# Output stores of a residual-quantizer codec kernel moved from GpSimd's queue to SyncE's, with retuned instruction order

## The chip, the cores and the metric

The kernel runs on one core of a Trainium2 chip. The metric is the device time of one execution in microseconds, from the first instruction to the last, of which the median over several executions is taken. One further execution was recorded by the hardware profiler, and all readings of engines, waits and transfers come from it.

## The reference

Two sequences of 16,000 frames with 512 channels pass through a three-tap depthwise filter and a SiLU. Then each frame is quantized in four rounds: find the nearest of eight codebook vectors, add it to the sum, subtract it from the residual. The sum passes through a second three-tap depthwise filter. All tensors are bf16.

```python
B, T, D, K = 2, 16000, 512, 3      # x: [B, T, D]; dw_enc, dw_dec: [K, D]
Nq, C = 4, 8                       # codebooks: [Nq, C, D]

xp = jnp.pad(x, ((0,0),(1,1),(0,0)))
z = sum(xp[:, i:i+T, :] * dw_enc[i] for i in range(K))      # (written as a loop)
z = jax.nn.silu(z)
res, q = z, 0
for s in range(Nq):
    cb = codebooks[s]
    d2 = |res|^2 - 2 res.cb + |cb|^2                        # [B, T, C]
    sel = cb[d2.argmin(-1)]
    q = q + sel
    res = res - sel
qp = jnp.pad(q, ((0,0),(1,1),(0,0)))
y = sum(qp[:, i:i+T, :] * dw_dec[i] for i in range(K))
```

## The kernel before

Each sequence is cut into tiles of up to 16 groups of 128 frames, 18 tiles in all. In a tile, partition p holds G neighbouring frames, so that a shift by one frame is a shift by one group slot. The channels have to lie on the partitions for the first filter; therefore x is loaded by transposing transfers, one for each group, and one more for each of the two halo slots at the ends (the frame before and the frame after). Two XT buffers take turns, so the load of tile n can begin when the taps of tile n - 2 have read their slots.

```python
SIZES = ([6, 8] + [16] * 7, [16] * 7 + [8, 6])
...
NX, NE, NZ, NOH, NY = 2, 3, 4, 4, 4          # buffers of XT, EX, Z, OHW, YB
...
def load(st):
    ...
    def one(g):
        nc.sync.dma_start_transpose(out=X[:, :, g + 1, :], in_=src[g])
    for g in range(G):
        add("SP", 1.56 if n < 2 else 1.36, ("load", n, 0.01 * g), lambda g=g: one(g), [], [("X", n % NX, g + 1)], tail=1.5)
    ...
    if t0 and n:       # halo in front: one more transposing transfer; else a memset and a copy on GpSimd
        ...
        add("SP", ..., lambda: nc.sync.dma_start_transpose(out=X[:, :, 0, :], in_=before), [], xe, tail=1.5)
    ...
```

In `front` the three taps are multiplied on VectorE (some on ScalarE) and added into Z; ScalarE makes the exponential, VectorE or ScalarE adds 1, ScalarE takes the reciprocal and VectorE multiplies it in (the SiLU). `select` computes the first three choices from scores (PE, VectorE), `resid` subtracts the three chosen vectors from Z in PSUM with one or two matmuls per block, after which either ScalarE copies the sum back (the matmul with the identity has added Z) or VectorE adds it to Z; then comes the fourth choice.

```python
def evac(zg=zg, box=box):
    v = ps(box)[:, 0:GH * P].rearrange("p (k c) -> p k c", c=P)
    if box["dest"] == "ACT":
        nc.scalar.copy(zg, v)
    else:
        nc.vector.tensor_tensor(out=zg, in0=zg, in1=v, op=ALU.add)
```

`windows` lays the one-hot choices of neighbouring frames beneath each other (OHW), and `back` makes the output from them by matmul with codebook times filter. ScalarE copies two groups at a time from PSUM into one of four YB buffers, and after two such copies the buffer is stored. The frames that two tiles share belong to one of them only; a store is therefore cut into pieces (112 partitions, 15 partitions, one partition and the like).

```python
def back(st):
    ...
    for k0 in range(0, GH, 2):
        ks = range(k0, min(k0 + 2, GH))
        y = ycount[0] % NY
        ycount[0] += 1
        Y = YB[y]
        for k in ks:
            ...
            add("ACT", act_psum(1024), key, lambda ...: nc.scalar.copy(Y[...], ps(box)), [], [("Y", y)], free=box, after=[j])
        add("POOL", 1.0, ("back", n, ks[-1] / GH), lambda Y=Y, g0=2 * k0, g1=2 * (ks[-1] + 1): store(st, Y, g0, g1), [("Y", y)], [],
            tail=5.0)

def store(st, Y, g0, g1):
    ...
    for p0, p1, lo, hi in split:
        nc.gpsimd.dma_start(out=view[p0:p1, lo:hi, :], in_=Y[p0:p1, lo - g0:hi - g0, :])
```

None of these calls issues at once. `add` notes a step with its engine, an assumed cost, its reads and writes and a rank; `Plan.order` then plays the steps through in a list scheduler with assumed costs and fixes the order in which every engine gets its instructions, and which engine takes the either-or steps. The weights `WHEN` set the rank of each kind of step in the first, the middle and the last tiles, `SHARE` and `SLACK` tilt the either-or choices, and `QUOTA` bounds how many PSUM blocks may wait for ScalarE or VectorE at a time. Where the scheduler sees PE idle it puts in filler matmuls (`fill`).

```python
rank = self.when[kind][part][0] + tile + self.when[kind][part][1] * place_in_tile      # shortened

def fill(j, k):
    for _ in range(k):
        nc.tensor.matmul(PS[j // 2][...], lhsT=IDENT, rhs=MSK.rearrange("p u w -> p (u w)"), start=True, stop=True)
```

Of the kernel before, what the change touches and what calls it, by code (L numbers as in the profile page):

```python
# [12 lines left out]
ACT = mybir.ActivationFunctionType  # L13
# [3 lines left out]
class Plan:  # L17
# [16 lines left out]
    def add(self, engine, cost, key, fn, reads=(), writes=(), take=None, free=None, hold=None, tail=0.0, after=(), dest=None, box=None, mm=0):  # L34
        n = len(self.steps)
        deps = set(after)
        for t in reads:
            if t in self.writer:
                deps.add(self.writer[t])
            self.readers.setdefault(t, []).append(n)  # L40
        for t in writes:
            if t in self.writer:
                deps.add(self.writer[t])
            deps.update(self.readers.get(t, ()))
            self.writer[t] = n
            self.readers[t] = []
        deps.discard(n)
        self.steps.append({"n": n, "e": engine, "c": cost, "k": key, "fn": fn, "deps": sorted(deps), "take": take, "free": free,
                           "hold": hold, "tail": tail, "dest": dest, "box": box, "mm": mm})
        return n  # L50
# [163 lines left out]
def kernel(  # L214
# [8 lines left out]
    nc = tc.nc  # L223
# [18 lines left out]
    PAIR = 1  # L242
    NX, NE, NZ, NOH, NY = 2, 3, 4, 4, 4
    NA = 4
    SHARE = (14.72, 0.75, -2.14)
    SLACK = (-0.24, -0.33, 0.67)
    QUOTA = {"ACT": 3, "DVE": 3}
    WHEN = {"setup": ((-0.151, 1.058), (0.208, 0.715), (-0.18, 0.669)), "load": ((-2.06, 0.878), (-1.99, 0.738), (-2.049, 0.878)),
            "pad": ((-1.379, 0.11), (-1.748, 0.188), (-2.303, 0.134)), "taps": ((0.021, 0.468), (-0.351, 0.479), (0.529, 1.222)),
            "exp": ((0.71, 0.323), (0.67, 0.275), (1.338, 0.094)), "plus1": ((1.243, 0.705), (0.347, 0.188), (-0.701, 0.508)),  # L250
            "recip": ((0.436, 0.72), (0.457, 0.028), (1.338, 0.536)), "gate": ((-0.006, 0.57), (0.836, 0.447), (1.306, 0.596)),
            "score0": ((-0.317, 0.008), (1.329, 0.132), (-0.226, 0.443)),
            "decide": ((1.768, 0.496), (0.086, 0.144), (0.22, 0.967)), "win0": ((2.207, 0.092), (2.21, 0.191), (2.978, 0.013)),
            "resid": ((1.259, 0.51), (1.669, 0.629), (1.801, 0.77)), "score3": ((2.134, 0.811), (2.579, 0.199), (3.141, 1.501)),
            "decide3": ((1.343, 0.361), (2.686, 0.74), (3.558, 0.652)), "win3": ((3.257, 0), (3.131, 1.109), (4.061, 0.121)),
            "back": ((2.863, 0.379), (3.366, 1.486), (4.147, 0.457))}
    assert B == len(SIZES) and T >= GM * P and GM <= 16

    xf = x.flatten_outer_dims()
# [65 lines left out]

    plan = Plan(NA, (3, len(tiles) - 3), SHARE, SLACK, QUOTA, WHEN)
    add = plan.add

    def ps(box):
        j = box["banks"][0]  # L330
        return PS[j // 2][:, 512 * (j % 2):512 * (j % 2 + len(box["banks"]))]
# [7 lines left out]
    def act_psum(n):  # L339
        return 0.055 + n / 1200  # L340

    def mm(n):
        return max(0.06, 0.004 + n / 2380)
# [398 lines left out]
    def back(st):  # L742
        n, GH = st["n"], st["GH"]
        W = OHW[n % NOH]
# [6 lines that stand above are left out]
                box = {}  # L751
                key = ("back", n, k / GH)

                def mms(k=k, box=box):
                    py = ps(box)
                    for u in range(2):
                        o = py[:, 512 * u:512 * u + 512]
                        wrap = (k == 0 and u == 0) or (k == GH - 1 and u == 1)
                        nc.tensor.matmul(o, lhsT=W[:, k, PADC:PADC + P], rhs=WDEC[u], start=True, stop=not wrap)  # L759
                        if wrap and u == 0:  # L760
                            nc.tensor.matmul(o, lhsT=W[:, GH - 1, PADC - 1:PADC - 1 + P], rhs=WDEC[2], start=False, stop=True)
                        elif wrap:
                            nc.tensor.matmul(o, lhsT=W[:, 0, PADC + 1:PADC + 1 + P], rhs=WDEC[3], start=False, stop=True)
                wraps = (k == 0) + (k == GH - 1)
                j = add("PE", (2 + wraps) * mm(512), key, mms, [("OHW", n % NOH, 0), ("OHW", n % NOH, 1)] + [("WDEC", v) for v in range(4)], [],
                        take=("A", box), dest="ACT", mm=2 + wraps)
                add("ACT", act_psum(1024), key, lambda k=k, box=box, Y=Y, k0=k0: nc.scalar.copy(  # L767
                    Y[:, 2 * (k - k0):2 * (k - k0) + 2, :].rearrange("p g d -> p (g d)"), ps(box)), [], [("Y", y)], free=box, after=[j])
            add("POOL", 1.0, ("back", n, ks[-1] / GH), lambda Y=Y, g0=2 * k0, g1=2 * (ks[-1] + 1): store(st, Y, g0, g1), [("Y", y)], [],
                tail=5.0)  # L770

    def store(st, Y, g0, g1):
        r0, a, e, G = st["row0"], st["a"], st["e"], st["G"]
        view = outf[r0:r0 + G * P, :].rearrange("(p g) d -> p g d", g=G)
        runs = []
        for p in range(P):
            lo = max(a - G * p, g0)
            hi = min(e - G * p, g1)
            if lo >= hi:
                continue  # L780
            if runs and runs[-1][2:] == [lo, hi]:
                runs[-1][1] = p + 1
            else:
                runs.append([p, p + 1, lo, hi])
        split = []
        for p0, p1, lo, hi in runs:
            m = (p1 - p0) // 16 * 16
            split += [(p0, p0 + m, lo, hi)] * (m > 0) + [(p0 + m, p1, lo, hi)] * (p0 + m < p1)
        for p0, p1, lo, hi in split:
            nc.gpsimd.dma_start(out=view[p0:p1, lo:hi, :], in_=Y[p0:p1, lo - g0:hi - g0, :])  # L790

    load(tiles[0])
    setup()
    for group in GROUPS:
        halves = {}
        for st in group:
            if st["n"]:
                load(st)
            for h in range(2):
                halves[st["n"], h] = front(st, h)  # L800
        for st in group:
            for h in range(2):
                front2(st, h, *halves[st["n"], h])
        for st in group:
            select(st)
            resid(st)
            back(st)
# [40 lines left out]
```

## Time and profile before

| what | value |
|---|---|
| median of 3 executions | 739.47 us (739.02 to 741.46) |
| span of the profiled execution | 739.7 us |
| mean granted TensorE clock | 0.949 |
| store issues on GpSimd (L790) | 130, 78.0 us busy |
| transposing loads on SyncE | 283 |
| data in the stores' queue | 32.78 MB in 10,640 packets |
| data in the loads' queue | 37.13 MB in 153,952 packets |
| time from a store's issue to its landing | 1.6 / 3.9 / 9.0 us (min / median / max) |

The profile's page gives for each engine its busy time and its share of the span; for groups of equal instructions the line, the engine, output and input, the count, the busy time and the mean duration; and the chain of work that ended last, followed back from the last instruction. "issue" stands for time in which an engine waited for nothing that the profile shows. PE is TensorE's matmul part, DVE is VectorE, ACT is ScalarE, POOL is GpSimd and SP is SyncE; a q behind the name is the engine's sequencer, which issues transfers. Durations of neighbouring instructions overlap a little, so their sum is above the busy time. Times behind a start are microseconds from the beginning of the span.

### The profile page before, as it was taken

How to read it: one execution, taken by the hardware profiler on the slowest of the kernel's cores; microseconds unless marked ns; L12 is line 12 of the kernel's file. 1: busy time of each engine (PE TensorE's matmuls, PEld its weight loads, DVE VectorE, ACT ScalarE, POOL GpSimd, SP SyncE). 2: the span in 40 equal slices, each digit the busy share in tenths (PEclk: the TensorE clock that was granted, in tenths of full speed). 3: DMA queues.
4: the chain of work that ended last, by engine and by line, in shares of the span. 5: the costliest groups of instructions: out<-in, count | busy, mean ns of one | idle time of the engine just before them, and what ended most of it. 6: DMA issues, size and time to landing. Idle time of an engine off the chain costs nothing.

```text
span 739.7 us, 24411 instructions
## 1 busy us (share of the span) xinstructions
PE 599.6 (81%) x10732; PEld 293.0 (40%) x10732; DVE 673.9 (91%) x1257; ACT 656.1 (89%) x584; POOL 90.0 (12%) x165
## 2 busy tenths in 40 slices
PE   5987977798689777876689969896788888899984
PEld 2443433345244333433245434443234444444441
DVE  8879798899999989998999999998799999899991
ACT  5677869899999979999899999999599999999664
POOL 2000000100040221103200011102101010201223
PEclk9998999899899999999899998999799999999997
DMA  5445544835182790629553292619523140203325
GB/s 112 91 98 130 101 89 86 133 69 88 30 187 44 117 179 8 131 62 182 95 101 74 54 184 72 109 50 209 111 57 87 37 91 2 88 32 115 116 84 182
DMA packets 164914, 71.89 MB, mean 97 GB/s; under 512 B 156640, under 2 KB 156672, under 8 KB 164808
## 3 DMA queue, kind: packets, MB, share of 16 engines
q1 hardware_dynamic: 153952, 37.13, 31.1%
q0 software_dynamic: 10640, 32.78, 14.5%
q8 instruction: 84, 1.38, 0.8%
q10 hardware_dynamic: 216, 0.43, 0.2%
q14 instruction: 22, 0.18, 0.1%
HBM read 0.43 MB, written 32.77 MB: 45 GB/s over the span
## 4 chain that ended last, share of the span: by engine, by line
DVE 52%; PE 20%; ACT 13%; issue 10%; DMA 2%; SPq 2%; POOL 1%; DVEq 0%; POOLq 0%; ACTq 0%
DVE ZB L710 12%; DVE ZB L365 9%; DVE TB L533 7%; ACT ZB L708 5%; PE ps L702 5%; DVE TA L365 5%; DVE TA L533 4%; PE ps L701 4%; PE ps L568 3%; PE ps L810 3%; ACT EX L550 3%; ACT EX L538 2%; DVE EX L540 2%; DVE OHW L679 2%; PE ps L759 2%
## 5 line engine op out<-in xcount | busy, mean ns | idle before, releaser
L702 PE MATMUL ps<-OHW,CBN 128*128 128x512 bf16 (+1 forms) x768 | 267.7, 387 | 14.8 <-DVE ZB L710 4.6
L708 ACT CAST ZB<-ps 128x1024 bf16<-128x1024 f32 (+2 forms) x290 | 248.8, 958 | 32.7 <-PE ps L702 32.5
L701 PE MATMUL ps<-ZB,IDENT 128*128 128x512 bf16 (+1 forms) x524 | 204.5, 390 | 22.2 <-DVE ZB L710 11.6
L710 DVE TENSOR_TENSOR ZB<-ZB,ps 128x1024 bf16<-128x1024 bf16 (+2 forms) x142 | 145.6, 1045 | 6.8 <-PE ps L702 6.1
L790 POOL DMA_DIRECT2D out_dram<-YB x130 | 78.0, 605 | 601.5 <-ACT YB L767 536.6
L767 ACT CAST YB<-ps 128x1024 bf16<-128x1024 f32 x126 | 123.1, 1052 | 12.8 <-PE ps L759 12.1
L538 ACT ACTIVATE EX<-ZB 128x4096 bf16<-128x4096 bf16 (+2 forms) x36 | 115.8, 3219 | 13.6 <-DVE ZB L365 13.5
L702 PEld LDWEIGHTS <-CBN 128*128 128x128 bf16 x768 | 75.9, 99 | 129.1 <-issue 61.1
L550 ACT ACTIVATE EX<-EX 128x4096 bf16<-128x4096 bf16 (+2 forms) x36 | 114.7, 3193 | 1.3 <-DVE EX L540 1.1
L568 PE MATMUL ps<-ZB 128*32 128x64 bf16 x8064 | 90.3, 197 | 13.8 <-issue 6.6
L568 PEld LDWEIGHTS <-ZB 128*32 128x32 bf16 x8064 | 76.9, 95 | 55.5 <-issue 52.8
L810 PE MATMUL ps<-MSK,IDENT 128*128 128x512 bf16 x307 | 81.2, 418 | 19.5 <-DVE RC L618 5.6
L533 DVE TENSOR_SCALAR TB<-XT,WENC 128x2048 bf16<-128x2048 bf16 (+2 forms) x140 | 94.1, 684 | 0.1
L759 PE MATMUL ps<-WDEC,OHW 128*128 128x512 bf16 x252 | 76.6, 395 | 13.1 <-DVE ZB L710 6.3
L701 PEld LDWEIGHTS <-IDENT 128*128 128x128 bf16 x524 | 52.5, 100 | 65.4 <-issue 13.8
L365 DVE TENSOR_TENSOR ZB<-ZB,EX 128x4096 bf16<-128x4096 bf16 (+2 forms) x36 | 72.6, 2019 | 3.7 <-ACT EX L550 3.7
L365 DVE TENSOR_TENSOR TA<-TA,TB 128x4096 bf16<-128x4096 bf16 (+2 forms) x36 | 72.7, 2018 | 0.1
L365 DVE TENSOR_TENSOR ZB<-TA,TB 128x4096 bf16<-128x4096 bf16 (+2 forms) x36 | 72.6, 2018 | 0.1
L810 PEld LDWEIGHTS <-IDENT 128*128 128x128 bf16 x307 | 30.9, 104 | 57.8 <-issue 31.0
L533 DVE TENSOR_SCALAR TA<-XT,WENC 128x2048 bf16<-128x2048 bf16 (+2 forms) x71 | 47.2, 682 | 0.2
L759 PEld LDWEIGHTS <-OHW 128*128 128x128 bf16 x252 | 23.3, 100 | 43.9 <-issue 22.2
L540 DVE TENSOR_SCALAR EX<-EX 128x4096 bf16<-128x4096 bf16 (+2 forms) x36 | 39.1, 1087 | 1.7 <-ACT EX L538 1.7
(100 smaller groups left out, 426.8 us busy)
## 6 DMA issues: line engine op xcount, KB each, us to landing
out_dram<-YB POOLq DMA_DIRECT2D x33, 448.0 KB, 3.8
out_dram<-YB POOLq DMA_DIRECT2D x28, 512.0 KB, 4.2
XT<-in_x_dram SPq DMA_TRANSPOSE x283
out_dram<-YB POOLq DMA_DIRECT2D x30, 60.0 KB, 4.7
out_dram<-YB POOLq DMA_DIRECT2D x31, 2.0 KB, 2.5
out_dram<-YB POOLq DMA_DIRECT2D x2, 224.0 KB, 3.9
YB<-in_dw_dec_dram ACTq DMA_DIRECT2D x1, 384.0 KB
out_dram<-YB POOLq DMA_DIRECT2D x1, 384.0 KB
```

Source lines behind the costliest of these rows:

```text
L365: add("DVE", cost, key, lambda: nc.vector.tensor_tensor(out=out, in0=a, in1=b, op=op), reads, writes, **kw)
L533: lambda dst=dst, src=src, w=w: nc.vector.tensor_scalar(out=dst, in0=src, scalar1=w, scalar2=None, op0=ALU.mult),
L538: add("ACT", act(2 * R), ("exp", n, h), lambda: nc.scalar.activation(v(ex), Z, ACT.Exp, scale=-1.0), zt, [("EX", sl), "ACTTAB"], hold="E")
L550: nc.scalar.add_instruction(mybir.InstActivation(name=nc.get_next_instruction_name(), engine=mybir.EngineType.Activation, func=ACT.Reciprocal,
L568: nc.tensor.matmul(o[HB * q:HB * (q + 1), u * ZW:(u + 1) * ZW].rearrange("p (s c) -> p s c", s=2), lhsT=blk, rhs=both, start=False, stop=( ...
L701: nc.tensor.matmul(o, lhsT=IDENT, rhs=zg[:, k0:k0 + nk, :], start=True, stop=False)
L702: nc.tensor.matmul(o, lhsT=CBN[s, u][:, i * P:(i + 1) * P], rhs=W[:, k0:k0 + nk, PADC:PADC + P], start=not on_act, stop=True)
L708: nc.scalar.copy(zg, v)
L710: nc.vector.tensor_tensor(out=zg, in0=zg, in1=v, op=ALU.add)
L759: nc.tensor.matmul(o, lhsT=W[:, k, PADC:PADC + P], rhs=WDEC[u], start=True, stop=not wrap)
L767: add("ACT", act_psum(1024), key, lambda k=k, box=box, Y=Y, k0=k0: nc.scalar.copy(Y[:, 2 * (k - k0):2 * (k - k0) + 2, :].rearrange("p g d ...
L810: nc.tensor.matmul(PS[j // 2][:, 512 * (j % 2):512 * (j % 2) + NMK * ZW], lhsT=IDENT, rhs=MSK.rearrange("p u w -> p (u w)"), start=True, s ...
```

## The change

The output stores are issued by SyncE, in the same queue as the transposing loads; GpSimd has nothing left to do after the setup but the few halo memsets and copies at the ends of the sequences. The loads and their halo slots are as before. [...]The scheduler's weights were tuned anew for the new queue (with 0.5 in place of 1.0 for a store's issue and 4.0 in place of 5.0 for its landing), so the order of instructions on all engines differs from before.

```diff
-    SHARE = (14.72, 0.75, -2.14)
-    SLACK = (-0.24, -0.33, 0.67)
-    QUOTA = {"ACT": 3, "DVE": 3}
-    WHEN = {"setup": ((-0.151, 1.058), (0.208, 0.715), (-0.18, 0.669)), "load": ((-2.06, 0.878), (-1.99, 0.738), (-2.049, 0.878)),
-            ... (all other kinds of steps)
+    SHARE = (19.5, 1.71, -1.34)
+    SLACK = (0.8, -4.83, -5.72)
+    QUOTA = {"ACT": 4, "DVE": 4}
+    WHEN = {"setup": ((-0.05, 1.675), (0.613, 1.016), (0.464, 0.931)), "load": ((-2.074, 0.741), (-2.063, 0.601), (-2.58, 0.741)),
+            ... (all other kinds of steps)
@@ back
-            add("POOL", 1.0, ("back", n, ks[-1] / GH), lambda Y=Y, g0=2 * k0, g1=2 * (ks[-1] + 1): store(st, Y, g0, g1), [("Y", y)], [],
-                tail=5.0)
+            add("SP", 0.5, ("back", n, ks[-1] / GH), lambda Y=Y, g0=2 * k0, g1=2 * (ks[-1] + 1): store(st, Y, g0, g1), [("Y", y)], [],
+                tail=4.0)
@@ store
-            nc.gpsimd.dma_start(out=view[p0:p1, lo:hi, :], in_=Y[p0:p1, lo - g0:hi - g0, :])
+            nc.sync.dma_start(out=view[p0:p1, lo:hi, :], in_=Y[p0:p1, lo - g0:hi - g0, :])
```

## The prediction

> **What bounds the kernel now.** I read the busy shares first. In the page's first part each engine has its busy time, its share of the span and its number of instructions:
>
> ```profile
> PE 599.6 (81%) x10732; PEld 293.0 (40%) x10732; DVE 673.9 (91%) x1257; ACT 656.1 (89%) x584; POOL 90.0 (12%) x165
> ```
>
> VectorE is busy 91% and ScalarE 89%: two engines share the bound. GpSimd, which the change empties, has 12%. VectorE's whole idle time is 739.7 - 673.9 = 65.8 us, which caps what a change can win that leaves VectorE its work. Next, the table by stretches (start:end, length, then busy time and instruction count of each engine, granted clock, DMA share, GB/s) says where the 65.8 us lie:
>
> ```profile
> 460.00:500.00 40.00, 34.74 (x785) 17.65 (x784) 39.84 (x52) 39.94 (x32) 3.90 (x6) 1.00 0.43 80
> 500.00:540.00 40.00, 27.23 (x510) 13.15 (x509) 33.04 (x78) 32.06 (x23) 6.87 (x13) 0.87 0.79 148
> 700.00:720.00 20.00, 17.91 (x274) 8.20 (x273) 18.28 (x48) 12.96 (x17) 3.62 (x7) 1.00 0.23 81
> 720.00:740.00 20.00, 8.66 (x134) 3.84 (x132) 4.81 (x14) 10.07 (x11) 7.80 (x15) 0.80 0.56 185
> ```
>
> 460 to 500 is the good middle: VectorE and ScalarE full. 500 to 540 is the worst middle stretch (7 us of VectorE idle). The last 20 us hold 15.2 us of VectorE idle: there the kernel only drains. Summing the same table, the first 100 us hold about 15 us, the last 40 about 17, the rest about 33.
>
> The chain that ended last says the same, and says how small the part of the changed engine is:
>
> ```profile
> DVE 52%; PE 20%; ACT 13%; issue 10%; DMA 2%; SPq 2%; POOL 1%; DVEq 0%; POOLq 0%; ACTq 0%
> ```
>
> GpSimd has 1% of it, about 7 us, SyncE's queue and the transfers 2% each. So stores cost the end nearly nothing until the tail. Then I read the two queues that the change joins. Issue durations (min/median/max ns) of the transposing loads on SyncE, of the store issues on GpSimd, and of one plain transfer issued by ScalarE through the same kind of queue as SyncE's:
>
> ```profile
> L494 SPq DMA_TRANSPOSE XT<-in_x_dram x252: 1188/1265/3319, 0.7 to 594.9; - x126
> L790 POOL DMA_DIRECT2D out_dram<-YB x130: 484/536/2732, 69.0 to 735.9; - x130
> L350 ACTq DMA_DIRECT2D YB<-in_dw_dec_dram x1: 356/356/356, 4.2 to 4.2; - x1
> ```
>
> SyncE's timeline in the middle shows its rhythm (start, length, instructions merged):
>
> ```profile
> 412.10 29.09 SPq L494 DMA_TRANSPOSE XT<-in_x_dram  x16
> 441.24 1.26 SPq L502 DMA_TRANSPOSE XT<-in_x_dram  x1
> 442.55 1.26 SPq L508 DMA_TRANSPOSE XT<-in_x_dram  x1
> 450.77 28.20 SPq L494 DMA_TRANSPOSE XT<-in_x_dram  x16
> ```
>
> One tile of 16 groups takes 18 issues; seven tiles from 198.19 to 490.59 us give a period of 41.8 us. Part of the 29 us is waiting: the chain of waits of SyncE has about 180 us of waits on VectorE (taps that still read the XT buffer) over the run. Last the tail, GpSimd's timeline:
>
> ```profile
> 723.97 1.57 POOL L790 DMA_DIRECT2D out_dram<-YB  x3 [1.53 <-ACT YB L767]
> 728.79 4.05 POOL L790 DMA_DIRECT2D out_dram<-YB  x8 [3.25 <-ACT YB L767]
> 735.43 1.07 POOL L790 DMA_DIRECT2D out_dram<-YB  x2 [2.58 <-issue]
> ```
>
> ScalarE's last copy starts at 731.1 and ends near 732.2; the last two stores issue only at 735.43, after 2.58 us [...], and the span ends at 739.7. The tail behind the last compute is 7.5 us.
>
> [...]issues have median 536 and maximum 2732 ns, so a few are held up, but no VectorE operation is: the 2048-element taps have a median of 746 and the longest tap into TB took 758 ns, into TA 894. [...]queue shares now are 31.1% (loads) and 14.5% (stores), which the change puts into one queue. [...]No run here shows SyncE stores yet. [...]The 180 us of SyncE waits are the reason why that may hurt.
>
> **The change part by part.** *Issue work.* 130 store issues leave GpSimd (78.0 us busy) and join SyncE's 283 transposes. At 0.36 us (the ScalarE sample) to 0.60 us (its slowest, the 3 KB load) they are 47 to 78 us on SyncE beside 283 x 1.265 = 358 us: 405 to 436 us, 55 to 59% of the span. Per period: 18 x 1.28 + 8 x 0.5 = 27 us of 41.8. SyncE isn't a bound by volume.
>
> *Order.* SyncE takes its list in order, so a store waits behind loads and a load behind stores. I compared the new SyncE order with its gates: for every load the last tap of the tile two before (in VectorE's order), for every store its last YB copy (in ScalarE's). Positions are sums of the mean durations of the rows by shape up to that instruction, each engine scaled to end near 720 to 725 us; read in the same way, before's stores come out 5 to 20 us ahead of the trace, both engines alike, so I shift both by 15. Example: the load of tile 10 stands behind the third store of tile 4. Store ready at 286 + 15 = 301, tap gate of tile 8 at 288 + 15 = 303: the store costs it nothing. The load then takes about 22 us to 325; tile 10's first tap stands at 337 + 15 = 352. Margin 27 us. Going through all 18 loads in this way, margins are 2 to 5 us for tiles 2 to 4 (no store ahead of them), about 15 for tiles 5 and 6, and 24 to 41 for tiles 7 to 17. From tile 3 on, a store that stands behind a load lags about 18 to 25 us, mostly one per tile, on the fourth YB buffer; that buffer is next written about 20 us after such a store. So neither side should close on the path: 0 us.
>
> *VectorE and ScalarE.* The two orders hold the same work but for flips of the either-or operations: VectorE gets 6 more OHW copies of 0.4 to 0.7 us and 5 more small OT copies, and loses 6 residual adds (4 x 0.68, 2 x 0.55) and some taps: -1 us. ScalarE gets 6 short casts, three short taps and one "plus 1" of 2048, and loses 6 OHW copies, 5 OT copies and a long tap: +1 us. PE loses 13 filler matmuls and gains 6 identity matmuls. Nothing here moves the bound.
>
> *Tail.* Only here are stores on the path. In the new order the last stores are again the pieces of the last two tiles. The issue of the last piece [...](3.2 us past the last copy) should shrink to about 1.5 as each issue is shorter [...]. I put it at -2 us (-1 to -3).
>
> *Retuned ranks.* Planner weights, the PSUM quota (3 to 4) and the store's assumed tail differ, so nearly every instruction has another place. The 33 us of middle idle can go either way. 13 fewer fillers mean that the planner saw a little less PE idle; I take -3 us from it, with a spread of 10.
>
> Sum: 739.5 - 2 - 3 + 0 = 734.5 us.
>
> **The rivals.** First, head-of-line blocking: ScalarE runs late, a store holds SyncE, and the next load is late for its taps. For it speaks that a store is placed ahead of most loads; against it the margins of 24 us and more. If half the 14 full tiles lost 3 us: +21, 758 us. Second, the opposite: a store stuck behind an 18-transpose load keeps a YB buffer and stops ScalarE. The trace has no ScalarE wait on a store among its listed waits, and one 2.64 us piece in the chain at 483.49; with lags of 18 to 25 us against reuse in about 20 to 30, a few waits of 1 to 3 us are possible: +5, 742 us. Third, GpSimd's silence frees VectorE. Against: VectorE durations show no tail; at most 1 us. Fourth, the retuned order fills the dips like 500 to 540: if half of the 33 us go, 718 us; nothing in the profile says that it must.
>
> **Range and chances.** The mechanical part is small and one-sided (-1 to -3); the reshuffle has about +-10, blocking a thin tail upwards. 8 in 10: 720 to 750. 2% is 14.8 us: faster means below 724.7, slower above 754.3. I give 0.18, 0.70 and 0.12.
>
> **What would show it.** Right: SyncE's loads keep a 1.26 us median, store issues on it take 0.35 to 0.6 us, no wait of VectorE's taps on XT transfers in the middle of the run, no YB wait on ScalarE beyond a few us, VectorE and ScalarE busy within 3 us of now, a tail behind the last copy of 5 to 6 us. Wrong: SyncE waiting on ScalarE's YB copies while VectorE idles for XT; landing times above 6 us as stores share a queue with transposes; store issues above 1 us, which would put SyncE near 70%; or a middle idle far from 33 us, which would be the reshuffle and not the stores.

## The result, and the profile after

The change makes the kernel 1.1% faster: 731.31 us median (730.0 to 732.07, four executions) against 739.25 us (736.4 to 741.46, four executions) of the kernel before in the same comparison, a ratio of 0.9893 with the interval 0.9856 to 0.993. The predicted time was 734.5 us with the range 720 to 750. As the runs below show, the size came out nearly right while the division of the sum between queue and order was wrong.

The profiled execution of the kernel after has a span of 729.5 us at a clock of 0.961. Busy times by engine, and the chain that ended last, on its page (its lines are numbered one lower than before: the store is L789, the load L493, the copy into YB L766):

```profile
PE 593.4 (81%) x10725; PEld 289.3 (40%) x10725; DVE 675.0 (93%) x1258; ACT 658.3 (90%) x583; POOL 10.7 (1%) x35
```

```profile
DVE 50%; PE 28%; ACT 10%; issue 8%; DMA 3%; SPq 1%; ACTq 0%; DVEq 0%
```

The work of VectorE and ScalarE is as before (+1.1 and +2.2 us); GpSimd has fallen from 90.0 to 10.7 us. So the 10.2 us between the two spans are idle time of VectorE that has gone: 729.5 - 675.0 = 54.5 us in place of 65.8. The table by stretches of the kernel after, in the columns of the prediction's table:

```profile
460.00:500.00 40.00, 31.71 (x443) 14.78 (x443) 38.78 (x64) 37.33 (x27) 0.00 (x0) 0.91 0.35 81
500.00:540.00 40.00, 33.46 (x714) 17.05 (x714) 37.29 (x62) 36.21 (x31) 0.00 (x0) 0.91 0.50 111
700.00:720.00 20.00, 18.75 (x309) 9.05 (x307) 16.36 (x42) 14.45 (x21) 0.00 (x0) 1.00 0.29 101
720.00:740.00 20.00, 1.90 (x8) 0.70 (x8) 0.23 (x1) 4.57 (x5) 0.00 (x0) 0.82 0.30 93
```

The worst middle stretch, 500 to 540, lost 7 us of VectorE before and loses 2.7 now; the best one lost 0.2 and loses 1.2. Next, the issue durations on SyncE (min/median/max ns, first and last start):

```profile
L493 SPq DMA_TRANSPOSE XT<-in_x_dram x252: 1189/1265/2552, 0.7 to 603.1; - x126
L789 SPq DMA_DIRECT2D out_dram<-YB x130: 227/370/1666, 96.5 to 725.1; - x130
```

The load's issue is unchanged (median 1.265 us). A store's issue takes 0.37 us where GpSimd took 0.54. SyncE's timeline shows what one queue means here: its 413 issues start one after another, none before the one ahead of it has ended, and stores and loads alternate in blocks.

```profile
404.66 12.97 SPq L789 DMA_DIRECT2D out_dram<-YB  x8
417.72 28.68 SPq L493 DMA_TRANSPOSE XT<-in_x_dram  x16
449.13 15.79 SPq L789 DMA_DIRECT2D out_dram<-YB  x12
```

Eight store issues of 0.4 us fill 13 us here because they wait for ScalarE's copies (8.8 us in three waits, the longest 6.7, and no load starts meanwhile). Last the tail, ScalarE's and SyncE's timelines:

```profile
715.94 10.50 SPq L789 DMA_DIRECT2D out_dram<-YB  x14
718.06 6.51 ACT L766 CAST YB<-ps 128x1024 bf16<-128x1024 f32 x7 [0.32 <-ACT YB L766]
```

The last copy ends at 718.06 + 6.51 = 724.6 us and the span at 729.5: a tail of 4.9 us, where it was 7.5. Before, GpSimd paused 2.58 us ahead of its last two issues; the profile names nothing that it waited for ("issue"), and what it was stays open. Here no such gap stands: SyncE's last two issues start at 724.4 and 725.1 us.

### The profile page after: what moved, and what is told of

Same layout as the page of the kernel before. It is cut to its first block, busy times and chain, and to the rows that moved or that the text cites. A ratio compares the mean times of both kernels' runs of the same rounds, so it can differ in the third digit from the quotient of the medians.

```text
span 729.5 us, 24386 instructions
## 1 busy us (share of the span) xinstructions
PE 593.4 (81%) x10725; PEld 289.3 (40%) x10725; DVE 675.0 (93%) x1258; ACT 658.3 (90%) x583; POOL 10.7 (1%) x35
## 3 DMA queue, kind: packets, MB, share of 16 engines
q8 instruction: 84, 1.38, 0.8%
## 4 chain that ended last, share of the span: by engine, by line
DVE 50%; PE 28%; ACT 10%; issue 8%; DMA 3%; SPq 1%; ACTq 0%; DVEq 0%
DVE ZB L709 12%; PE ps L701 8%; DVE ZB L364 7%; PE ps L700 7%; DVE TA L364 6%; DVE TB L532 6%; PE ps L567 5%; ACT YB L766 3%; DVE TA L532 3%; PE ps L758 3%; ACT ZB L707 2%; DVE EX L539 2%; DVE OHW L678 2%; PE ps L809 2%; ACT EX L549 1%
## 5 line engine op out<-in xcount | busy, mean ns | idle before, releaser
L707 ACT CAST ZB<-ps 128x1024 bf16<-128x1024 f32 (+2 forms) x296 | 253.5, 933 | 33.1 <-PE ps L701 32.0
L709 DVE TENSOR_TENSOR ZB<-ZB,ps 128x1024 bf16<-128x1024 bf16 (+2 forms) x136 | 143.0, 1063 | 4.7 <-PE ps L701 4.2
L766 ACT CAST YB<-ps 128x1024 bf16<-128x1024 f32 x126 | 121.8, 1045 | 9.0 <-PE ps L762 4.1
L567 PEld LDWEIGHTS <-ZB 128*32 128x32 bf16 x8064 | 75.2, 95 | 55.9 <-issue 52.4
L567 PE MATMUL ps<-ZB 128*32 128x64 bf16 x8064 | 87.5, 197 | 7.0 <-issue 4.2
L532 DVE TENSOR_SCALAR TB<-XT,WENC 128x2048 bf16<-128x2048 bf16 (+2 forms) x139 | 92.6, 684 | 0.2
L758 PE MATMUL ps<-WDEC,OHW 128*128 128x512 bf16 x252 | 74.0, 387 | 13.5 <-DVE ZB L709 4.5
L809 PE MATMUL ps<-MSK,IDENT 128*128 128x512 bf16 x294 | 73.7, 402 | 13.5 <-DVE RC L617 2.4
L700 PEld LDWEIGHTS <-IDENT 128*128 128x128 bf16 x530 | 53.0, 100 | 67.6 <-issue 15.9
L809 PEld LDWEIGHTS <-IDENT 128*128 128x128 bf16 x294 | 28.9, 102 | 47.5 <-issue 19.9
L758 PEld LDWEIGHTS <-OHW 128*128 128x128 bf16 x252 | 22.8, 98 | 41.7 <-issue 18.4
L561 PE MATMUL ps<-MSK,IDENT 128*128 128x512 bf16 (+1 forms) x64 | 24.5, 383 | 8.5 <-ACT ZB L707 2.4
```

The lines of the kernel that those rows point to most:

```text
L532: lambda dst=dst, src=src, w=w: nc.vector.tensor_scalar(out=dst, in0=src, scalar1=w, scalar2=None, op0=ALU.mult),
L567: nc.tensor.matmul(o[HB * q:HB * (q + 1), u * ZW:(u + 1) * ZW].rearrange("p (s c) -> p s c", s=2), lhsT=blk, rhs=both, start=False, stop=( ...
L700: nc.tensor.matmul(o, lhsT=IDENT, rhs=zg[:, k0:k0 + nk, :], start=True, stop=False)
L809: nc.tensor.matmul(PS[j // 2][:, 512 * (j % 2):512 * (j % 2) + NMK * ZW], lhsT=IDENT, rhs=MSK.rearrange("p u w -> p (u w)"), start=True, s ...
```

## The experiments

The change has two parts, the queue of the stores and the order of instructions. The first question was which of the two brought the 8 to 10 us. The theory followed the prediction: the queue moves only the tail, the retuned order does the rest. The rival: the queue does more than the tail, in the middle. Each ratio is to the kernel before as it ran in the same comparison: 740.82 us for the first four runs, 740.26 for the four with thin stores, 739.57 for the last four. One profiled execution stands behind each reading of idle time.

**Each part alone.** The order of before with all stores on SyncE:

```diff
-            nc.gpsimd.dma_start(out=view[p0:p1, lo:hi, :], in_=Y[p0:p1, lo - g0:hi - g0, :])
+            nc.sync.dma_start(out=view[p0:p1, lo:hi, :], in_=Y[p0:p1, lo - g0:hi - g0, :])
```

> The kernel before with its own order of PE, VectorE and ScalarE to the last instruction; only the 130 stores are issued by SyncE, merged into its loads by planned time. Theory (the queue is worth only its tail, the rest of the 8 us is the retuned order): about 736.5 us, ratio 0.995 to 0.998, the stretch behind ScalarE's last copy 5 us in place of 7.5. Rival 1 (the queue gives it all): 731 to 732, ratio 0.989. Rival 2 (an order that was not planned for it blocks SyncE): above 739.5, with VectorE waiting for XT.

The order of after with all stores on GpSimd (the same edit the other way round, in the kernel after):

> The changed kernel with its order of PE, VectorE and ScalarE to the last instruction; only the stores go back to GpSimd. Theory: about 734 us, ratio 0.992 to 0.995, tail again 7 to 7.5 us, the last copy still ends near 725 to 727. Rival 1 (the queue gives it all): 739. Rival 3 (the new order needs the freed buffers of the new queue): above 736 with ScalarE waiting for YB.

And the kernel after once more, in the same comparison:

> The changed kernel unchanged, on the same chip as the two halves: 731 us, ratio 0.989. Theory: its gain is the sum of the gains of the two halves within 2 us; if stores and order need each other, it is more than the sum.

Measured, with 740.82 us for the kernel before: queue alone 730.79 us, ratio 0.9861 (0.9838 to 0.9884); order alone 733.24 us, 0.9886 (0.9856 to 0.9916); both 731.48 us, 0.9871 (0.9845 to 0.9897). Either part alone gives the whole gain. If the two were independent, both together would give 0.9861 x 0.9886 = 0.975; the measured interval ends far above that. The two parts therefore remove for the most part the same loss. And the queue alone brings 10 us, of which the tail (7.5 to 5.5 us in this run) is only 2.

The order's part has a second rival, TensorE's granted clock: on average 0.963 in the six executions of the order alone, against 0.955 in the 27 of the kernel before and 0.956 in the six of the queue alone. Among those 27 a clock higher by 0.01 went with 2.1 us less (interval 0.5 to 3.7), so up to 3 of the order's 8 us may come with the clock. The queue's 10 us don't. No run held the clock fixed.

**Tail and middle apart.** The order of before, with the stores of the last two tiles on SyncE, and then its complement, all stores but those:

```diff
-            nc.gpsimd.dma_start(out=view[p0:p1, lo:hi, :], in_=...)
+            (nc.sync if st["n"] >= len(tiles) - 2 else nc.gpsimd).dma_start(...)     # last two tiles
+            (nc.sync if st["n"] < len(tiles) - 2 else nc.gpsimd).dma_start(...)      # the complement
```

> The kernel before, in which only the stores of the last two tiles are issued by SyncE. Theory: the same gain as with all stores on SyncE, 736.5 to 737.5, ratio 0.995 to 0.998, since only the tail of the stores is on the path. Rival: under 1 us of gain, so that any gain of all stores on SyncE comes from the middle.

> The order of the kernel before, with every store but those of the last two tiles on SyncE: the complement of the run that moved only the last two tiles' stores. Theory (the middle and the tail are separate gains): the whole queue change brought about 10 us, its tail part about 2, so this run should lie 7 to 8 us below the kernel before, ratio 0.988 to 0.992, with a tail behind the last copy of about 7 us as before. Rival (the gain of the middle is drift of the runs, or hangs on the tail's queue): within 3 us of before, ratio above 0.996.

Measured: the last two tiles alone 738.9 us, ratio 0.9973 (0.995 to 0.9995), with a tail of 5.2 us behind the last copy; the complement 733.89 us against 739.57, ratio 0.9915 (0.9885 to 0.9944), with a tail of 7.0 us. 0.9973 x 0.9915 = 0.9888, just above the queue's own interval (0.9838 to 0.9884) and in agreement with it by the spread of the two pieces. So the queue's gain does consist of two pieces, about 2 us in the tail and 6 to 8 us in the middle. The middle piece isn't in the prediction.

Where in the middle? The table by stretches, of the kernel before:

```profile
300.00:400.00 100.00, 77.44 (x1709) 39.07 (x1694) 95.44 (x149) 95.06 (x70) 12.21 (x16) 0.95 0.60 114
500.00:600.00 100.00, 78.73 (x1568) 38.98 (x1567) 90.31 (x165) 90.90 (x72) 10.30 (x21) 0.91 0.49 99
```

Of the same order with all stores on SyncE:

```profile
300.00:400.00 100.00, 81.37 (x1745) 40.43 (x1744) 99.07 (x154) 98.07 (x74) 0.00 (x0) 0.95 0.54 109
500.00:600.00 100.00, 81.62 (x1641) 40.47 (x1640) 92.60 (x167) 93.43 (x75) 0.72 (x2) 0.91 0.43 100
```

VectorE idles 4.6 and 9.7 us in these stretches before, 0.9 and 7.4 with the other queue. VectorE's whole idle time between 100 and 680 us, from such tables of each run (580 less the busy times), puts all runs side by side. The thin stores are explained below.

| order, queue of the stores | idle 100 to 680 us | tail behind the last copy |
|---|---|---|
| before, GpSimd (the kernel before) | 33.0 | 7.5 |
| before, only last two tiles on SyncE | 29.4 | 5.2 |
| before, all but these on SyncE | 23.9 | 7.0 |
| before, SyncE | 24.4 | 5.5 |
| after, GpSimd | 22.8 | 7.5 |
| after, SyncE (the kernel after) | 22.8 | 4.9 |
| before, GpSimd, thin stores | 26.9 | 6.6 |
| before, SyncE, thin stores | 24.1 | 2.5 |
| after, GpSimd, thin stores | 20.7 | 6.7 |
| after, SyncE, thin stores | 18.8 | 2.5 |
| before, GpSimd, six output buffers (below) | 28.2 | 7.6 |
| after, SyncE, six output buffers (below) | 22.5 | 5.1 |
| after, only last two tiles on SyncE (below) | 23.8 | 5.6 |
| after, SyncE, second comparison | 24.9 | 5.1 |

The queue takes 33.0 to 24.4 with the old order and leaves 22.8 at 22.8 with the new one. That is the missing additivity in one view. One caution: single profiles scatter. Those with two tiles moved (span 733.3 us, median 738.9) and with six buffers (736.2 and 741.28) were quicker than their kernels' medians, so 29.4 and 28.2 are low; and the kernel after gave 22.8 and 24.9.

**Bytes or issues?** The middle loss could come from the stores' bytes, whose packets take 14.5% of the time of the 16 DMA engines beside the loads' 31.1%, or from their issues and GpSimd's own work. The same four kernels were run with thin stores: as many issues to the same frames' first rows, but 64 bytes per partition in place of up to 4 KB. The issues stay 130; in GpSimd's queue the packets fall with the bytes, from 10,640 to 4,160 (in SyncE's they stay 9,694). The rest of the output is left out, so these are not usable kernels.

```diff
-            nc.gpsimd.dma_start(out=view[p0:p1, lo:hi, :], in_=Y[p0:p1, lo - g0:hi - g0, :])
+            nc.gpsimd.dma_start(out=view[p0:p1, lo:lo + 1, 0:32], in_=Y[p0:p1, lo - g0:lo - g0 + 1, 0:32])
```

The order of before, GpSimd:

> The kernel before, in which each of the 130 store issues on GpSimd writes 64 bytes per partition in place of up to 4 KB; the rest of the output is left out. As many issues [...], but 1/64 of the bytes or less. Theory now (what costs in the middle is the stores' bytes meeting the transposing loads on the 16 DMA engines[...]): the middle gain of the queue change comes without touching the queue: 731 to 734 us, ratio 0.988 to 0.993. Rival [...]: 738 or more, ratio above 0.996.

The order of before, SyncE:

> The same cut of bytes with all stores on SyncE and the order of before. Theory: little is left to gain, 728 to 731 us, and the gap to thin_before is only the tail, 2 to 3 us. Rival (SyncE's queue gains by itself): 7 us or more below thin_before.

The order of after, GpSimd:

> The same cut with the retuned order and stores on GpSimd. Theory (the retuned order gains only because its stores meet fewer loads): within 2 us of thin_before. Rival (the retuned order is shorter by itself): 4 to 7 us below thin_before.

The order of after, SyncE:

> The same cut in the changed kernel. Theory: within 2 us of thin_a, 728 to 731. Rival (two gains that add once collisions are gone): 4 us or more below thin_a.

Measured ratios to the kernel before with its full stores, and those of the full stores again:

| | GpSimd | SyncE |
|---|---|---|
| order before, full | 1 | 0.9861 (0.9838 to 0.9884) |
| order after, full | 0.9886 (0.9856 to 0.9916) | 0.9871 (0.9845 to 0.9897) |
| order before, thin | 0.9900 (0.9853 to 0.9947) | 0.9824 (0.9781 to 0.9866) |
| order after, thin | 0.9871 (0.9821 to 0.992) | 0.9798 (0.9755 to 0.9841) |

Without the bytes the two parts become additive: from the thin kernel before, the queue gives 0.9824 / 0.9900 = 0.9923, the order 0.9871 / 0.9900 = 0.9971, and the product 0.9900 x 0.9923 x 0.9971 = 0.9795 is what both gave, 0.9798. By the mean times of the runs, the gain that both parts share is 9.8 us with full stores and 0.3 with thin ones, each within about 3. Hence what they share is a loss by the bytes. In microseconds (ratio differences times 740) the bytes cost the kernel before 7.4, queue alone 2.7, order alone 1.1, both 5.4; with intervals of some 4 us on each, only the first and the last stand clear of nothing. In the new order the bytes cost no less on SyncE than on GpSimd, so one queue isn't cheaper for them in every order. And not all of the queue's gain is bytes: with thin stores it still gives 6.3 us in the old order, not the 2 to 3 expected, and 4.1 of them are the tail (6.6 to 2.5 us). The thin kernel before, with GpSimd still issuing, idles as little in 300 to 400 and 500 to 600 as the SyncE queue does:

```profile
300.00:400.00 100.00, 79.64 (x1680) 39.78 (x1679) 98.50 (x155) 97.24 (x73) 10.12 (x13) 0.95 0.45 70
500.00:600.00 100.00, 81.40 (x1645) 40.43 (x1645) 92.64 (x169) 93.34 (x72) 12.16 (x20) 0.91 0.27 44
```

95.44 went to 98.50 of 100 and 90.31 to 92.64. All profiles of the old order show how firm each place is (idle us of VectorE):

| stretch | GpSimd, full: before, two tiles moved, six buffers | SyncE: all, all but two tiles | thin: GpSimd, SyncE |
|---|---|---|---|
| 100 to 300 | 11.9, 9.9, 9.0 | 9.2, 9.3 | 11.2, 10.5 |
| 300 to 400 | 4.6, 4.7, 1.6 | 0.9, 1.6 | 1.5, 0.7 |
| 500 to 600 | 9.7, 8.9, 10.4 | 7.4, 7.1 | 7.4, 7.5 |

500 to 600 separates the groups, by some 2 us; 300 to 400 does so in two of three executions, by 3; 100 to 300 not at all. So some 2 to 5 us have a place, and the rest of the 6 to 8 us of the middle has none that single profiles can show. The kernel after still pays for bytes in one place, 500 to 600; of the kernel after:

```profile
500.00:600.00 100.00, 84.91 (x1838) 42.31 (x1838) 94.78 (x152) 93.42 (x77) 2.71 (x2) 0.95 0.44 105
```

and of the same with thin stores:

```profile
500.00:600.00 100.00, 84.91 (x1912) 43.04 (x1912) 98.20 (x163) 97.17 (x79) 3.16 (x2) 0.98 0.28 46
```

3.4 us there and 2.4 us of tail (4.9 against 2.5) make 5.8, close to its 5.4 us. The place is less firm than the sum: the order alone, whose bytes cost 1.1 us in all, idles 5.0 us there, and 1.9 with thin stores.

**What a collision looks like.** Of the kernel before, two stretches of 4 us, in which a store overlaps loads (DMA shares above 1 count packets that are open at the same time):

```profile
344.00:348.00 4.00, 2.21 (x90) 1.61 (x78) 2.73 (x5) 3.97 (x4) 1.77 (x3) 1.00 1.88 209
348.00:352.00 4.00, 1.90 (x89) 1.32 (x88) 1.28 (x3) 2.71 (x1) 0.00 (x0) 0.70 0.83 233
```

VectorE loses 4 of 8 us. Its table of waits from 344 to 352 us (total, times, longest) names what it waited for, and what that waited for:

```profile
DVE PR L623 <- PE ps L568: 3.5, 1, 3.5
PE ps L568 <- issue: 3.5, 1, 3.5
```

VectorE needs scores from PE, and PE stands still for 3.5 us with nothing that the profile shows to wait for. The queues from 345 to 352 us (packets, MB, share):

```profile
q1 hardware_dynamic: 2561, 0.62, 102.1%
q0 software_dynamic: 255, 0.71, 35.4%
q8 instruction: 2, 0.03, 2.0%
```

Loads and stores together keep the engines full (102.1% + 35.4%), and two packets of the instruction queue lie among them. With the stores on SyncE the corresponding place, some 2 us earlier, reads

```profile
346.00:350.00 4.00, 2.33 (x73) 1.12 (x71) 4.00 (x7) 4.00 (x3) 0.00 (x0) 1.00 1.45 97
```

and VectorE loses nothing. The tempting reading, that PE's next instructions came late, would be a guess. The trace shows the instruction queue (84 packets, 1.38 MB in the run) and the stall beside a full set of engines. It doesn't show that the stall waits for such a packet, nor for which engine a packet is: the one that moved within the stall (347.3 to 348.3 us) took 1.04 us, no longer than usual (median 1.01), and PE stood for 1.4 us more. The DMA engines are nearly as full in the SyncE run (packet time 126% from 343 to 350 us, here 139.5% from 345 to 352), so load alone isn't it. Nor does the stall come each time: in the profile with six buffers, the same order and queue, the longest such wait of PE between 340 and 360 us was 1.6 us. What PE stood still for is not shown.

What can be measured is how long stores and loads run side by side. In the traces a load's packets have 256 bytes and a store's mostly 4 KB. The time in which packets of both kinds (256 bytes; 2 KB and more) are open is 43 us before (44 with six buffers), 21 with the queue alone, 28 with the order alone and 6 in the kernel after. Either part sets the stores where they meet fewer loads, and one issuer for both doesn't keep them fully apart (21 and 6 us). The gain doesn't grow with it: from 21 or 28 down to 6 the kernel becomes no faster. Which moves of the new order do this, no run singled out.

The sum of all packets' times falls too, but says less than it seems to. The queue shares of the order of before with SyncE, and of the kernel after:

```profile
q1 hardware_dynamic: 163646, 69.90, 42.9%
```

```profile
q1 hardware_dynamic: 163646, 69.90, 41.1%
```

In microseconds of all 16 engines: before 31.1% + 14.5% of 739.7 = 337, queue alone 42.9% of 729.1 = 313, order alone 29.5% + 13.9% of 730.7 = 317, after 300. Now the old order with thin stores, on GpSimd and then on SyncE:

```profile
q1 hardware_dynamic: 153952, 37.13, 30.0%
q0 software_dynamic: 4160, 0.53, 1.1%
```

```profile
q1 hardware_dynamic: 163646, 37.66, 28.4%
```

30.0% + 1.1% of 732.2 = 228 us falls to 28.4% of 726.2 = 206. The queue takes 22 us off the sum without the stores' bytes and 24 with them, so this fall isn't made by the bytes, and it is no measure of the loss. What makes it stays open.

**Output buffers.** Could a late landing, holding a YB buffer, be the loss in place of the DMA engines? Six output buffers in place of four, order and queue unchanged:

```diff
-    YB = [sb([P, 4, D], BF16, f"YB{b}") for b in range(NY)]
+    YB = [sb([P, 4, D], BF16, f"YB{b}") for b in range(NY + 2)]
-            Y = YB[y]
+            Y = YB[(ycount[0] - 1) % (NY + 2)]
```

> The kernel before with six output buffers in place of four, instruction order and queue unchanged; a copy then waits for a store six back and not four back. Theory (bytes of stores against loads in the DMA engines, not waits on output buffers, cost the middle): within 2 us of before, ratio 0.997 to 1.003. Rival (ScalarE waits in the middle for a landing that is late): 4 us or more faster, ratio below 0.995.

> The kernel after with six output buffers in place of four, order and queue unchanged. Theory: copies of ScalarE no longer wait for stores that stand behind 18 loads in SyncE's queue (in the kernel after the longest such wait at a copy was 4.4 us); 1 to 3 us faster than the kernel after, ratio 0.983 to 0.987. Rival (those waits lie beside other work): the same as after, ratio 0.987 to 0.990.

Measured: before with six 741.28 us against 739.57, ratio 1.0021 (1.0 to 1.0042); after with six 730.95 us, 0.9884 (0.9848 to 0.992). Neither gains. In the kernel before the buffers aren't the loss. The longest semaphore wait at a copy into YB, 8.4 us at 343 us, stands there with six buffers too (8.0 us), so it isn't for a buffer. In the kernel after the longest was 4.4 us; with six buffers none is above 3.5, and the time is the same: that wait lay beside other work, as the rival had it.

**The tail with the new order.** The order of after, only the last two tiles' stores on SyncE (the same edit as above, in the kernel after):

> The order of the kernel after, with only the last two tiles' stores on SyncE and all others on GpSimd. Theory (with the new order the middle gains nothing from the queue, only the tail does): about 2 us below the run with this order and all stores on GpSimd, so ratio about 0.986, as fast as the kernel after or a little faster. Rival (queue and order give their gains in one and the same place, the tail): no better than that run, ratio 0.989 or above.

Measured: 733.13 us against 739.57, ratio 0.9899 (0.9863 to 0.9935), no better than the same order with GpSimd throughout (0.9886). The tail in its profile did shrink, from 7.5 to 5.6 us, but the last copy ended at 726.0 in place of 723.2 us: VectorE lost 1.7 us more in the first 100 us and 1.0 more in the middle. The interval is wide enough to hide the 2 us. This stays open; what the queue gives in the new order is known only from the full change (731.48 against 733.24 us, intervals overlapping).

## Why the prediction was right, and where it was not

**What bounds the kernel.** Right. VectorE's work is unchanged, the gain is idle time, and it stayed inside the cap of 65.8 us.

**Issue work.** Right. 283 loads at 1.265 us and 130 stores at 0.37 us are 406 us on SyncE, the lower end of the 405 to 436; loads kept their 1.265 us and stores lie in the 0.36 to 0.60 us taken from the one sample of ScalarE's queue, with a maximum of 1.67.

**Order.** The margins held: VectorE's taps wait 0.4 us in the whole run for XT transfers, in one wait. Rival one, head-of-line blocking (758 us), is gone. Rival two, a buffer stuck behind a load (742 us), is gone too: a few such waits exist, and six buffers in place of four take nothing off. (Added to the prediction's own 734.5 us, their 21 and 5 us give 755.5 and 739.5.) But from "neither side closes on the path" the prediction concluded **0 us** for the queue in the middle, and this step failed. With the old order the queue takes 8.6 us of VectorE's idle time out of the middle (4 to 5 when set against the two quicker profiles), and the run with all stores but the last tiles' moved gained 6 us in time, in executions enough for an interval of 0.9885 to 0.9944. The prediction weighed what the two lists of one issuer do to each other. It didn't ask what the transfers of two issuers do to each other: before, packets of stores and loads were open together for 43 us, with one issuer for 21, and the loss that queue and order share is gone once the stores' bytes are (9.8 us with full stores, 0.3 with thin ones). By which path the bytes stop VectorE stays open. One issuer for inputs and another for outputs brought nothing here: two queues against one are 740.8 against 730.8 us in the old order and 733.2 against 731.5 in the new.

**VectorE and ScalarE.** -1 and +1 us were predicted, +1.1 and +2.2 came; nothing moved. Rival three, VectorE freed by GpSimd's silence (at most 1 us): nothing to see, the long taps have a median of 746 ns in both traces.

**Tail.** Right in size, half right in its working: -2 (-1 to -3) predicted, 7.5 to 4.9 = -2.6 in the profile and, for the last two tiles alone, 0.27% or 2 us in time. The issues did move up: the last one starts 0.5 us behind the last copy (725.1 against 724.6) where it started 3.7 behind (735.9 against 732.2). Shorter issues (0.37 us against 0.54) are the smaller part of that: the pause of 2.58 us is gone, and it wasn't a wait for an earlier store's bytes (last section). From the last issue's start to the end it is 4.4 us, before 3.8: nothing was won there.

**Retuned ranks.** -3 us with a spread of 10. The order alone brought 0.9886 (8 us), so within the spread, but the reason given, 13 fewer fillers, can explain little of it: with thin stores the order gives 0.9971, some 2 us. By the thin runs, most of its gain is again the bytes of the stores, which meet fewer loads in this order (28 us side by side against 43).

**The sum.** -2 - 3 + 0 = -5 was predicted and about -8 measured. That it came near is luck: each part alone gives more than was put down for it, the queue some 7 us in the middle in place of 0 and the order 8 in place of 3, and these two share one gain: in the kernel after, the order had already taken what the queue would have. The idle time of 100 to 680 us went from 33.0 to 22.8 us (the first 100 us gave back 2.5). Rival four (718 us, half of the 33 us gone) had the place right, the middle's dips such as 500 to 540, and a third of the 33 us went in place of half; but the new order wasn't needed for it, the queue alone fills nearly as much.

**Signs named.** Loads' median, store issues, taps without waits, busy times within 3 us and buffer waits of a few us all came as listed, the tail at 4.9 a little below "5 to 6". Of the signs of being wrong, one came: a middle idle far from 33 us (22.8), "which would be the reshuffle and not the stores". The run with the old order and SyncE, at 24.4 us, shows that this reading was wrong. SyncE did wait for YB copies, 224 us in all, but VectorE didn't idle for XT meanwhile. Single store issues passed 1 us (up to 1.67), the median didn't. Landing times of SyncE's stores aren't in this trace.

## What to carry to other kernels

In this kernel two issuers whose transfers ran at once for 43 us went with a loss (740.8 us, with one issuer 730.8) although the queues took only 31.1% and 14.5% of the DMA engines' time, and in the stall above no wait named a transfer: look in short stretches where the DMA share is above 1 (1.88 there) and an engine stops for "issue" (3.5 us). Before tuning an order around such a dip, try one issuer for both kinds (here 10 us with the old order, nothing clear of noise with the new one), and shrink the bytes of one kind as a test. Two changes that each bring 1% may be the same 1%; run each alone before adding them up.

## What the runs showed that was not expected

**The tail on GpSimd's queue isn't transfer time.** With 64 bytes per partition it hardly shrank (7.5 to 6.6 us). GpSimd's and ScalarE's timelines of the kernel before with thin stores:

```profile
719.05 6.51 ACT L767 CAST YB<-ps 128x1024 bf16<-128x1024 f32 x7 [1.98 <-PE ps L759]
722.19 4.09 POOL L790 DMA_DIRECT2D out_dram<-YB  x8 [4.36 <-ACT YB L767]
728.77 1.07 POOL L790 DMA_DIRECT2D out_dram<-YB  x2 [2.50 <-issue]
```

The last copy ends at 725.6, the span at 732.2. The pause of 2.50 us ahead of the last two stores is that of the full stores (2.58), so that pause doesn't wait for the stores' bytes; what it waits for isn't shown. With SyncE (same order, thin) the tail is 2.5 us; with full stores 6.6 and 2.5 become 7.5 and 5.5. On SyncE 3.0 of the 5.5 us are bytes, on GpSimd 0.9 of 7.5.

**One long stall, hidden in the averages.** A single stop of PE of 3.5 us, up to 349.7 us, made VectorE lose 4 us. It stood in the profiles of the kernel before and (3.0 us, up to 346.7 us) of the one with two tiles' stores moved, but not in that with six buffers, and in none with all stores on SyncE. On the page it is only part of a sum, the 6.6 us of "issue" ahead of that line's matmuls.
